# Squares of the first three FFN groups moved to ScalarE, and w_out rounded in pieces of two blocks

## The chip, the core and the metric

The kernel runs on one core of a Trainium2 chip. The metric is the device time of one execution in microseconds. The kernel before was run three times: 516.62, 516.91 and 517.46 us, median 516.91. One further execution was profiled; its time is 516.3 us, and the span from its first to its last instruction, which every time in the profile refers to, is 514.5 us. The five engines are named as in the profile: PE is TensorE (PEld its weight loads), DVE is VectorE, ACT is ScalarE, POOL is GpSimd, SP is SyncE, which issues nearly all DMAs.

## What is computed

An mLSTM cell, step by step over 768 positions for 4 batches and 8 heads of width 40, followed by a feed-forward network whose activation is the squared rectifier:

```python
for t in range(S):
    m_new = np.maximum(f_gate[:, :, t] + m, i_gate[:, :, t])
    f_stab, i_stab = np.exp(f_gate[:, :, t] + m - m_new), np.exp(i_gate[:, :, t] - m_new)
    C = f_stab[:, :, None, None] * C + i_stab[:, :, None, None] * np.einsum('bhd,bhe->bhde', vt, kt)
    n = f_stab[:, :, None] * n + i_stab[:, :, None] * kt
    ...
    y[:, :, t] = o * h_tilde / denom
x = y.transpose(0, 2, 1, 3).reshape(3072, 320)
h = np.maximum(x @ w_in, 0.0)          # w_in: 320 x 2048
out = h * h @ w_out                    # w_out: 2048 x 320
```

The weights w_in and w_out arrive as 8-byte words, of which the kernel makes 4-byte floats on the chip.

## The kernel before

The 3072 rows are 24 tiles of 128 positions, six for each batch. The recurrence is worked in chunks: for a tile s, scores(s) are products of keys and queries on TensorE, weigh(s) makes the decay weights from exponentials on ScalarE (after mask(s) on GpSimd), weighted(s) multiplies scores and weights on VectorE (line 438), attend(s) or attend_turned(s) takes the result times the values on TensorE (lines 461, 513, 522), and normalise(s) divides on VectorE (lines 585 to 593, or 568 to 577) and leaves a tile x_sb. For tiles 0 to 5 turn_rows(s) transposes x_sb on TensorE (line 623) and ScalarE copies the result from PSUM to xT (line 624). For later tiles this goes through DRAM.

The FFN works on groups of two tiles, twelve in all. Groups 0, 1 and 2 are computed in the plain way: ffn1_main and ffn1_rest multiply xT by w_in (lines 645 and 656) in four parts of four blocks of 128 hidden units, two PSUM tiles `h_ps` to a part. relu_half (line 671) takes both to SBUF tiles `r_sb` on ScalarE, and square_half (line 678) squares them on VectorE into `g4`, a part of the group's tile g2. ffn2 multiplies that by w_out (line 685). From group 1 on the second product, and from group 3 on the first, use a scheme with seven products in place of eight (lines 739, 813, 845); in groups from 3 on ScalarE already squares (lines 862, 863). `h_ps` has three buffers in the first phase and five in the second.

The weights are converted by the class Rounding, piece by piece: fetch issues the load of a raw piece on SP's queue, words makes two tiles from its two words on ScalarE (lines 196, 198), join works on these with three VectorE operations (lines 207, 211, 212) and one GpSimd addition that writes the weight (line 216), and then fetches the piece four further on. words runs one piece ahead. There are 10 pieces of w_in, 512 wide, and 16 of w_out, 320 wide. `raw` has four buffers, `mag` and `low` three each.

The order on every engine is the order of the program text: the schedule is written out by hand. The first phase is the loop over u = 0 to 7 at line 956, two steps for each of the tiles 2 to 5; it computes FFN parts of groups 0 and 1, and each step begins with relu_half for the part of the step before. square_half stands after weigh in even steps and at the end of odd ones. The table NEXT says how many pieces are to be joined by the end of each step. Behind the loop stand, in this order, relu_half, square_half and turn_rows(5). The second phase is the loop over `parts` at line 1028, from group 2's first product on, with tile s = 6 + n // 4; LAST does there for n = 0 to 4 what NEXT did. Parts of group 2 come in pairs: both are multiplied, and then relu_half and square_half are called for one and for the other.

Of the kernel before, what the change touches and what calls it, by code (L numbers as in the profile page):

```python
# [9 lines left out]
F32 = mybir.dt.float32  # L10
I32 = mybir.dt.int32
U32 = mybir.dt.uint32
BF16 = mybir.dt.bfloat16
AF = mybir.ActivationFunctionType
ALU = mybir.AluOpType
PSUM = bass.MemoryType.PSUM

P = 128
# [11 lines left out]
def kernel(  # L30
# [27 lines left out]
    nc = tc.nc  # L58
# [7 lines left out]
    DM = H * D  # L66
    DFF = moe_w_in.shape[1]
    NF = DFF // P
# [4 lines left out]
    WG = GT * P  # L73
# [17 lines left out]
    conv = brought.enter_context(tc.tile_pool(name="conv", bufs=2, side="right"))  # L91
# [23 lines left out]
    w_out = consts.tile([P, NF, DM], F32)  # L115
# [27 lines left out]
    def in_words(ap):  # L143
        return ap.bitcast(I32).rearrange("r (c w) -> r c w", w=2)

    win_w, wout_w = in_words(moe_w_in), in_words(moe_w_out)

    rest = win_w[2 * P :].rearrange("p (a two f) w -> p a two f w", two=2, f=P)
    pieces = []
# [8 lines left out]
            ))  # L158
    IN_DONE = (3, 5, 8, 10)
    assert len(pieces) == IN_DONE[-1]  # L160
    pieces += [(w_out[:, fb, :], [(slice(0, P), wout_w[fb * P : (fb + 1) * P])]) for fb in range(NF)]
    NRAW = 4

    class Rounding:
# [11 lines left out]
        def fetch(self):  # L176
            n = len(self.raws)
            if n == len(pieces):
                return
            dst, srcs = pieces[n]  # L180
            raw = conv.tile([P, 512, 2], I32, name="raw", bufs=NRAW)
            self.raws.append(raw)
            for rows, src in srcs:
                to = raw[rows, : dst.shape[1]]
                if len(src.shape) == 4:
                    to = to.rearrange("p (a f) w -> p a f w", a=src.shape[1])
                nc.sync.dma_start(to, src)

        def words(self):
            n = len(self.a)  # L190
            if n == len(pieces):
                return
            w = pieces[n][0].shape[1]
            raw = self.raws[n][:, :w]
            mag = conv.tile([P, 512], F32, name="mag", bufs=3)
            nc.scalar.activation(mag[:, :w], raw[:, :, 1].bitcast(F32), AF.Abs)
            low = conv.tile([P, 512], F32, name="low", bufs=3)
            nc.scalar.activation(low[:, :w], raw[:, :, 0].bitcast(U32), AF.Copy, bias=2.0, scale=2.0 ** -51)
            self.a.append((mag, low))

# [67 lines left out]
    st = {}  # L268
# [51 lines left out]
    def load_o(s):  # L320
        b, c = divmod(s, NB)
        r, (s0, s1) = next((r, (a, z)) for r, (a, z) in enumerate(RUNS) if a <= s < z)
        if s == s0:
            st["og", r] = ld.tile([P, 4, H, D], F32, name="og")
        og = st.setdefault(s, {})["og"] = st["og", r][:, s - s0]
        nc.sync.dma_start(og, o_gate[b, :, c * P : (c + 1) * P, :].rearrange("h p d -> p h d"))
# [338 lines left out]
    def relu_half():  # L665
        if "half" in st:
            hs, g4 = st.pop("half")
            rs = []
            for h in hs:
                rs.append(ffn.tile([P, 2, WG], F32, name="r_sb", bufs=4))  # L670
                nc.scalar.activation(rs[-1][:], h[:], AF.Relu)
            st.setdefault("relu", []).append((rs, g4))

    def square_half():
        if st.get("relu"):
            rs, g4 = st["relu"].pop(0)
            for i, r in enumerate(rs):
                nc.vector.tensor_tensor(g4[:, :, i, :], r[:], r[:], op=ALU.mult)

    def ffn2(g, j, part):  # L680
        if part == 0:
# [212 lines left out]
    load_part(0, 0)  # L894
    load_part(0, 1)
    fetch(2)
    make_consts()
    load_part(1, 0)
    load_part(1, 1)
    load_part(0, 2)  # L900
    fetch(1)
    load_o(0)
    load_o(1)
    load_part(1, 2)
    fetch(1)
    idle(12)
    transposes(0)
# [16 lines left out]
    ffn = ctx.enter_context(tc.tile_pool(name="ffn", bufs=2))  # L924
# [27 lines left out]
    rounding.step()  # L952


    NEXT = (5, 8, 10, 11, 13, 15, 17, 19)
    for u in range(8):
        s = 2 + u // 2
        relu_half()
        if u % 2 == 0:
            if u == 0:  # L960
# [10 lines left out]
            if u == 2:  # L971
                mask(s + 1)
                rounding.join()
                rounding.join()
                weigh(s + 1, masked=True)
                rounding.words()
            else:
                weigh(s + 1)
                square_half()
        else:  # L980
# [7 lines left out]
            if u == 3:  # L988
                square_half()
# [10 lines left out]
            rounding.words()  # L1000
            ffn1(u // 4, u % 4)
            square_half()
        if u < 4:
            load_o(4 + u)
        while rounding.done < NEXT[u]:
            rounding.step()
    relu_half()
    square_half()
    turn_rows(5)
# [12 lines left out]
    for g in range(1, NG):  # L1022
        parts += [(2, g, i) for i in range(4)]
        if g + 2 < NG:
            parts += [(1, g + 2, i) for i in range(4)]
    LAST = (21, 23, 25, 25, 26)
    assert LAST[-1] == len(pieces)
    for n, (which, g, i) in enumerate(parts):
        s, at = 6 + n // 4, n % 4
# [46 lines left out]
        if fast:  # L1076
            (ffn1_close if i % 2 else ffn1_open)(g, i // 2)
            if at == 2:
                do(scale_q, s + 1)
        elif which == 1:  # L1080
            ffn1_main(g, i)
            if i % 2 == 0:
                held = st["half"]
            else:

                both = held, st["half"]
                for more, half in enumerate(both):
                    ffn1_rest(g, i - 1 + more, half[0])
                for half in both:
                    st["half"] = half  # L1090
                    relu_half()
                    square_half()
        elif g == 0:
            ffn2(g, *divmod(i, 2))
        else:
            ffn2_fast(g, i)
# [13 lines left out]
        if n < 5:  # L1110
            while rounding.done < LAST[n]:
                rounding.step()
# [30 lines left out]
```

## Time and profile before

| what | us |
|---|---|
| time, median of three runs | 516.91 |
| span of the profiled execution | 514.5 |
| VectorE squares, line 678, 24 of 128x512 | 18.6 |
| ScalarE relus, line 671, 24 of 128x512 | 12.7 |
| ScalarE words, lines 196 and 198, 26 each | 29.3 |
| VectorE rounding, lines 207, 211, 212, 26 each | 43.9 |
| GpSimd additions, line 216, 26 | 27.6 |
| landing of a 320 KB piece of w_out, median | 3.4 |

These are busy times over the whole span. They say how much work of each kind there is, not what it costs: an engine's work adds to the span only where TensorE or the end of the program waits for it. In the list of instructions in order of time a row gives the start, the length, the engine, the line, the operation, the tiles written and read, the shapes and, in brackets, how long the engine stood idle before it and what ended that. The first relu of line 671 starts at 44.1 us and the last square of line 678 ends at 125.4 us.

### The profile page before, as it was taken

What the parts mean: (1) busy time and instruction counts of PE and PEld (TensorE: products, weight loads), DVE (VectorE), ACT (ScalarE), POOL (GpSimd) and SP (SyncE); (2) the same over time, 40 slices, a digit from 0 to 9 for tenths busy, and PEclk for the clock granted to TensorE, in tenths of its full rate; (3) what the DMA queues carried; (4) which work ended last, traced back from release to release, by engine and by line L of the source; (5) the groups of instructions that cost most, each with busy time, mean ns of one, the idle gap of its engine ahead of it and who ended that gap; (6) DMA issues with size and microseconds to landing.
All of it is one profiled execution on the core that took longest, in us unless ns stands there. A gap on an engine that the chain in (4) does not pass through costs nothing.

```text
span 514.5 us, 11947 instructions
## 1 busy us (share of the span) xinstructions
PE 504.2 (98%) x4649; PEld 462.4 (90%) x4649; DVE 367.6 (71%) x678; ACT 238.1 (46%) x496; POOL 117.1 (23%) x146
## 2 busy tenths in 40 slices
PE   9989999999999999999999999999999999999997
PEld 4867878886698999999999999999999999999997
DVE  8589988969979776677777776677667766544441
ACT  3766667642522642571551581550771651432400
POOL 3345733233314113112112112112112121020000
PEclk9997999999999999999999999999999999999999
DMA  9999599787485786685685685685665352100000
GB/s 191 220 219 194 155 164 204 178 183 145 121 162 102 169 151 118 163 162 109 161 157 114 164 155 118 166 172 96 169 131 99 109 120 74 51 8 29 0 27 27
DMA packets 238360, 67.64 MB, mean 131 GB/s; under 512 B 185728, under 2 KB 232832, under 8 KB 238304
## 3 DMA queue, kind: packets, MB, share of 16 engines
q1 hardware_dynamic: 238208, 66.68, 61.0%
q8 instruction: 37, 0.61, 0.5%
q10 hardware_dynamic: 96, 0.20, 0.1%
q14 instruction: 19, 0.16, 0.1%
HBM read 54.56 MB, written 17.86 MB: 141 GB/s over the span
## 4 chain that ended last, share of the span: by engine, by line
PE 89%; DVE 4%; DMA 2%; ACT 2%; issue 2%; SPq 1%; DVEq 0%
PE h_ps L739 33%; PE h_ps L813 23%; PE h_ps L845 7%; PE h_ps L645 5%; PE tp L423 4%; PE numT L522 3%; PE h_ps L685 3%; PE hp L461 2%; PE numT L513 2%; PE h_ps L656 1%; PE tp L411 1%; PE dC L454 1%; PE A_ps L352 1%; DMA num_rows<-tn 1%; PE dC L532 1%
## 5 line engine op out<-in xcount | busy, mean ns | idle before, releaser
L361 POOL TENSOR_SCALAR_AFFINE_SELECT A_bc<-A_bc 128x1024 f32<-128x1024 f32 x22 | 26.3, 1197 | 207.9 <-ACT kq L371 152.8
L739 PE MATMUL h_ps<-T,S 128*128 128x160 f32 x352 | 51.4, 299 | 0.0
L739 PE MATMUL h_ps<-w_out,g 128*128 128x160 f32 x336 | 49.2, 303 | 0.0
L371 ACT ACTIVATE kq<-A_bc 64x512 f32<-64x512 f32 x30 | 18.9, 628 | 65.2 <-DMA A_bc<-a_rows 65.0
L739 PEld LDWEIGHTS h_ps<-T,S 128*128 128x128 f32 x352 | 49.0, 190 | 0.0
L385 ACT ACTIVATE A_bc<-A_bc,b_T 128x128 f32<-128x128 f32 x144 | 44.1, 389 | 8.7 <-POOL A_bc L361 8.2
L739 PEld LDWEIGHTS h_ps<-w_out,g 128*128 128x128 f32 x336 | 46.1, 190 | 1.1
L645 PE MATMUL h_ps<-xT,w_in 128*128 128x256 f32 x192 | 45.9, 395 | 0.6 <-ACT xT L624 0.6
L645 PEld LDWEIGHTS h_ps<-xT,w_in 128*128 128x128 f32 x192 | 37.1, 198 | 6.6 <-ACT xT L624 0.9
L755 DVE TENSOR_TENSOR y_sb<-y_sb,h_ps 128x160 f32<-128x160 f32 x44 | 14.0, 319 | 38.5 <-PE h_ps L739 38.5
L813 PE MATMUL h_ps<-xT,w_in 128*128 128x128 f32 x288 | 40.6, 284 | 0.0
L826 ACT COPY r_sb<-h_ps 128x512 f32<-128x512 f32 x18 | 10.5, 584 | 63.0 <-PE h_ps L813 62.9
L813 PE MATMUL h_ps<-xs,w_in 128*128 128x128 f32 x288 | 38.0, 275 | 0.0
L813 PEld LDWEIGHTS h_ps<-xT,w_in 128*128 128x128 f32 x288 | 34.9, 191 | 2.8 <-issue 0.5
L845 PE MATMUL h_ps<-xT,w_in 64*128 64x128 f32 x432 | 36.9, 280 | 0.0
L845 PEld LDWEIGHTS h_ps<-xT,w_in 64*128 64x128 f32 x432 | 33.4, 187 | 2.2
L813 PE MATMUL h_ps<-xs,WS 128*128 128x128 f32 x288 | 35.1, 275 | 0.0
L813 PEld LDWEIGHTS h_ps<-xs,w_in 128*128 128x128 f32 x288 | 35.1, 192 | 0.0
L813 PEld LDWEIGHTS h_ps<-xs,WS 128*128 128x128 f32 x288 | 33.6, 192 | 0.0
L850 DVE TENSOR_TENSOR r_sb<-r_sb,h_ps 128x512 f32<-128x512 f32 x18 | 12.4, 687 | 26.0 <-PE h_ps L845 25.7
L739 PE MATMUL h_ps<-w_out,g_c 128*128 128x160 f32 x192 | 28.0, 302 | 0.0
L423 PE MATMUL tp<-kqT 40*128 40x128 f32 x384 | 27.0, 280 | 0.0
(167 smaller groups left out, 1071.2 us busy)
## 6 DMA issues: line engine op xcount, KB each, us to landing
A_bc<-a_rows SPq DMA_DIRECT2D x22, 512.0 KB, 4.6
raw<-in_moe_w_out_dram SPq DMA_DIRECT2D x16, 320.0 KB, 3.4
num_rows<-tn SPq DMA_DIRECT2D x18, 256.0 KB, 3.5
kq<-num_rows SPq DMA_DIRECT2D x72, 64.0 KB, 2.3
kqT<-kq_rows SPq DMA_DIRECT2D x34, 128.0 KB, 3.2
raw<-in_moe_w_in_dram SPq DMA_DIRECT2D x8, 512.0 KB, 5.5
kq<-in_k_dram SPq DMA_DIRECT2D x24, 160.0 KB, 4.9
va<-in_v_dram SPq DMA_DIRECT2D x24, 160.0 KB, 5.2
```

Source lines behind the costliest of these rows:

```text
L361: nc.gpsimd.affine_select(A[:], A[:], compare_op=ALU.is_ge, fill=-1e30, base=0, pattern=[[0, H], [1, P]], channel_multiplier=-1,)
L371: nc.scalar.activation(e[rows], st[s]["A"][0][rows, PR * i : PR * (i + 1), :], AF.Exp)
L385: nc.scalar.activation(d["W"][:, i * n + h, :], A[i][:, h, :], AF.Exp, bias=b_T[:, b, c, i * n + h : i * n + h + 1],)
L423: nc.tensor.matmul(sc[i][:, j, :], lhsT=d["kT"][rows, j, :], rhs=d["qT"][rows, j, :], start=True, stop=True,)
L522: nc.tensor.matmul(numT[i][halves[g], e, :], lhsT=va_w[s % NKQ][:, h * D1 : h * D1 + DP], rhs=d["P"][h % 2][:, h // 2, :] if s < KQ_SQ els ...
L645: nc.tensor.matmul(hs[i][:, n, :], lhsT=w_in[:, a, fb * P : (fb + 1) * P], rhs=xT[:, :, a, :], start=(n == 0 and a == 0), stop=False,)
L685: nc.tensor.matmul(o_ps, lhsT=st["g2", g][:, fb, j * P : (j + 1) * P], rhs=w_out[:, fb, :], start=(fb == 0), stop=(fb == NF - 1),)
L739: nc.tensor.matmul(to, lhsT=lhsT[:, p], rhs=rhs[:, p, :], start=(start and p == 0), stop=(p == NPAIR - 1), skip_group_check=True,)
L755: add = lambda to, a, b: nc.vector.tensor_tensor(to, a, b, op=ALU.add)
L813: nc.tensor.matmul(to[:, n, :], lhsT=lhsT[:, 4 * q + n, :], rhs=rhs, start=(start and n == 0), stop=True, skip_group_check=True,)
L845: nc.tensor.matmul(to[:, n, :], lhsT=w_in2[rows, 4 * q + n, :], rhs=rhs, start=False, stop=True, skip_group_check=True,)
L850: tt(U2[:], U2[:], Y[:], op=ALU.add)
```

## The change

relu_half writes the rectified values straight into `g4`, the tile that is to hold the squares, instead of into `r_sb`. square_half then squares all of `g4` in place by one ScalarE instruction of 128x1024, where two VectorE instructions of 128x512 squared `r_sb` into it. The places at which both are called stay. This holds for the three groups that use these functions.

The pieces of w_out take two blocks of 128 rows each, so there are 8 of 640 columns instead of 16 of 320. The buffers raw, mag and low grow from 512 to 640 columns. The tables NEXT and LAST are written for the new count: by the end of the first loop 15 of 18 pieces are joined (before, 19 of 26), and the last is joined at n = 2 of the second loop (before, at n = 4).

```diff
-    pieces += [(w_out[:, fb, :], [(slice(0, P), wout_w[fb * P : (fb + 1) * P])]) for fb in range(NF)]
+    pieces += [
+        (
+            w_out[:, fb : fb + 2, :].rearrange("p a d -> p (a d)"),
+            [(slice(0, P), wout_w[fb * P : (fb + 2) * P].rearrange("(a p) c w -> p a c w", p=P))],
+        ) for fb in range(0, NF, 2)
+    ]
+    WIDE = 2 * DM
...
-            raw = conv.tile([P, 512, 2], I32, name="raw", bufs=NRAW)
+            raw = conv.tile([P, WIDE, 2], I32, name="raw", bufs=NRAW)
...
-            mag = conv.tile([P, 512], F32, name="mag", bufs=3)
+            mag = conv.tile([P, WIDE], F32, name="mag", bufs=3)
...
-            low = conv.tile([P, 512], F32, name="low", bufs=3)
+            low = conv.tile([P, WIDE], F32, name="low", bufs=3)
...
             hs, g4 = st.pop("half")
-            rs = []
-            for h in hs:
-                rs.append(ffn.tile([P, 2, WG], F32, name="r_sb", bufs=4))
-                nc.scalar.activation(rs[-1][:], h[:], AF.Relu)
-            st.setdefault("relu", []).append((rs, g4))
+            for i, h in enumerate(hs):
+                nc.scalar.activation(g4[:, :, i, :], h[:], AF.Relu)
+            st.setdefault("relu", []).append(g4)
...
         if st.get("relu"):
-            rs, g4 = st["relu"].pop(0)
-            for i, r in enumerate(rs):
-                nc.vector.tensor_tensor(g4[:, :, i, :], r[:], r[:], op=ALU.mult)
+            g4 = st["relu"].pop(0)
+            nc.scalar.activation(g4, g4, AF.Square)
...
-    NEXT = (5, 8, 10, 11, 13, 15, 17, 19)
+    NEXT = (5, 8, 10, 11, 12, 13, 14, 15)
...
-    LAST = (21, 23, 25, 25, 26)
+    LAST = (16, 17, 18, 18, 18)
```

## The prediction

> **What bounds the kernel now.** First the busy shares and the forty slices of the page. TensorE's matmul row is full nearly everywhere, so the span is TensorE's own work plus the places where it waits; what the other engines are given or spared counts only there.
>
> ```profile
> PE 504.2 (98%) x4649; PEld 462.4 (90%) x4649; DVE 367.6 (71%) x678; ACT 238.1 (46%) x496; POOL 117.1 (23%) x146
> PEld 4867878886698999999999999999999999999997
> DVE  8589988969979776677777776677667766544441
> ```
>
> The weight-load row (PEld) shows the gaps better than the matmul row, whose ends are modelled: slices 4 to 12 (39 to 155 us) have holes, the later ones hardly any. The change acts between 44 and 128 us, in slices 4 to 10. So second I read the time-ordered list of weight loads there; in brackets stands the idle time before a row and what ended it.
>
> ```profile
> 65.75 0.73 PEld L656 LDWEIGHTS h_ps<-xT,w_in 64*128 64x128 f32 x8 [0.33 <-issue]
> 68.01 0.31 PEld L623 LDWEIGHTS tp<-ident,x_sb 128*128 128x128 f32 x3 [1.54 <-ACT r_sb L671]
> ...
> 99.53 3.32 PEld L645 LDWEIGHTS h_ps<-xT,w_in 128*128 128x128 f32 x16 [0.16 <-ACT xT L624]
> ...
> 126.20 0.42 PEld L513 LDWEIGHTS numT<-kq,C 40*64 40x64 f32 x14 [1.50 <-DVE A_bc L438]
> ```
>
> Only two gaps in this stretch exceed 0.5 us: before turn_rows(3) at 68.01, and at 126.20. Gaps of 0.33 us ended by "issue" stand at every such change of matmul shape and are normal. Third, VectorE's list, to see who made those gaps:
>
> ```profile
> 60.16 2.35 DVE L678 TENSOR_TENSOR g<-r_sb 128x512 f32<-128x512 f32 x2
> 62.44 0.85 DVE L207 TENSOR_SCALAR mag<-mag 128x320 f32<-128x320 f32 x1
> 63.33 0.92 DVE L211 TENSOR_SCALAR mag<-mag 128x320 int32<-128x320 int32 x1
> 64.28 0.49 DVE L212 SCALAR_TENSOR_TENSOR mag<-raw,mag 128x320 int32<-128x320 int32 x1
> ...
> 67.93 0.20 DVE L593 COPY x_sb<-x_sb 128x64 f32<-128x64 f32 x1
> ...
> 122.27 3.16 DVE L678 TENSOR_TENSOR g_c<-r_sb 128x512 f32<-128x512 f32 x4
> 125.46 1.29 DVE L438 TENSOR_TENSOR A_bc<-tp,A_bc 128x512 f32<-128x512 f32 x2
> ```
>
> VectorE runs without a pause from 60.16 to 68.1: two squares, one rounding piece, then normalise(3), whose last copy (67.93) frees the transposes of turn_rows(3). The profile puts that gap down to ScalarE's L671, but those relus ended at 68.05 by chance; the data waited for is x_sb. At 125.46 weighted(7) stands behind four squares, which themselves waited for relus; TensorE's numT needs the PSUM bank that weighted(7) frees. Both gaps are thus VectorE's queue, with squares in it.
>
> **What the Trainium skill says.** "ScalarE: Activation LUTs", section What ACT_TABLE_LOAD costs: an ACTIVATE with immediate operands takes 186 ns + 0.833 ns per element, and neighbours overlap by some 93 ns. For 1024 elements this gives 1039 ns; the trace has the square of L863 at 1043. "SBUF — State Buffer", section SBUF: two separate sides: VectorE and GpSimd share a port pair as an exclusive lock, and the later one blocks. The trace agrees: L211 takes 0.33 us at 119.83, but 0.92 at 63.33, where it ends just after GpSimd's L480 (63.19 to 64.07). "TensorE: Matmul & The Clock Gate", section What's actually happening: TensorE's clock falls to half after an idle window of about 3.4 us. The trace shows a half-clock stretch from 42 to 48.8 us, after weight loads had paused for 1.38 us at 38.5, so here less than a whole idle window preceded it.
>
> ```profile
> 42.00:44.00 2.00, 2.00 (x12) 2.00 (x12) 1.70 (x4) 2.00 (x9) 0.00 (x0) 0.50 1.16 287
> ```
>
> (The column after the engines is the granted clock: 0.50.)
>
> **The change part by part.** The order of instructions on TensorE is the same before and after; on ScalarE no table load is added.
>
> Removed from VectorE: 24 L678, 12.9 + 5.7 = 18.6 us by the two groups. Removed from the queue ahead of normalise(3): 2.35 us; ahead of weighted(7): 3.16 us plus their wait for the relus.
>
> Added to ScalarE: 12 squares of 128x1024 at 1.045 us, 12.5 us. Rounding of w_out: 320-wide ACTIVATEs follow each other every 0.39 us, 512-wide every 0.57, so 0.00092 us per element and 0.69 for 640: 32 x 0.39 = 12.5 becomes 16 x 0.69 = 11.0. VectorE's three operations together step by 1.13 us at 320 and 1.52 at 512, so 1.78 at 640: 16 x 1.13 = 18.1 becomes 8 x 1.78 = 14.2, where no lock lengthens them. GpSimd's joining add: 0.89 at 320, 1.34 at 512, about 1.6 at 640, 14.2 becomes 12.8. On SP 16 fetches become 8, each with twice the bytes; a bare issue is 0.34, so the queue is spared 2.7 us. All of this lies beside TensorE's work except at three places:
>
> 1. *turn_rows(3), gain.* Without the two squares VectorE goes from L472 (ends 60.2, set by TensorE's dC) straight to a 640-wide piece. Alone that takes 1.8 us, under the lock perhaps 3.1 (the 320-wide one took 2.26 instead of 1.13, and up to two GpSimd operations may be in the way). normalise(3), 3.4 us before, starts at 62 to 63.3 instead of 64.7 and ends by 66.7. TensorE can first use it at 66.81 (last L656 load ends 66.48, plus the normal 0.33). Gain 68.01 - 66.81 = 1.20 at most; if the lock costs everything, 0. I take 1.20.
>
> 2. *xT of tile 5, loss.* After the loop relu_half and square_half stand ahead of turn_rows(5). Before, ScalarE ran two relus and then the copy that ffn1 of group 2 waits for:
>
> ```profile
> 98.02 1.09 ACT L671 ACTIVATE r_sb<-h_ps 128x512 f32<-128x512 f32 x2 [2.33 <-PE h_ps L656]
> 99.00 0.48 ACT L624 COPY xT<-tp 128x384 f32<-128x384 f32 x1
> ```
>
> The relus cannot start earlier, since they waited for TensorE. Now the square (1.045) lies between, and it waits for the relus' end, so the 0.09 overlap is lost there but had again after it: the copy ends at 100.55 instead of 99.48, and TensorE, which already waited 0.16 for it, starts L645 about 1.05 later. Nothing else is queued that TensorE could do first. Loss 1.05; bounds 0.95 and 1.25.
>
> 3. *weighted(7), gain.* Before it now stand rounding piece 18, whose words ScalarE finishes by about 115.3 (relus from 109.7; two relus, square, two relus, square = 4.2, then two 640-wide words 1.4), and normalise(6), which waits for the num_rows loads (116.0). Both are done by 119, and scores(7) end on TensorE at 119.9. So L438 runs at 120 to 121.2, well before 124.5, where numT is first asked for. Its other input, ScalarE's exponentials, ends at 115.3 + 2.45 = 117.8. Gain 1.50, lower bound 1.2, upper 1.75 (part of the 0.44 gap before it).
>
> Other waits that squares lengthen on ScalarE have room: relus before which it idled 1.3 to 2.3 us (74.40, 83.52) take a square of 1.05; at 90.19 the relu comes 0.9 later, but TensorE asks for its bank at 93.5. With five banks in group 2, squares between relus hold a bank 1 us longer, asked for at 111.9 at the earliest. The fetches of 640 KB issued from 49 to 59 us put up to 1.3 MB more ahead of A_bc of tile 5, at 200 GB/s up to 6.5 us in all but only the last one or two still in flight, 1.6 to 3 us; weigh(5) feeds scores at 84, so that is hidden. After 128 us VectorE is again tied to TensorE, so the later gap near 165 moves along unchanged.
>
> Sum: -1.20 + 1.05 - 1.50 = -1.65 us on the profiled span of 514.5, to 512.85. The same execution counts 516.3 as its time, 1.8 more; the three runs give 516.62 to 517.46, median 516.91. I apply the difference to the median: **515.3**. The bounds of the three terms add up to -2.0 and +0.05, 514.9 to 517.0; the upper end is the lock case below. With at least 0.8 of the first gain kept, the forecast's own range is 514.9 to 516.2.
>
> **Rivals.** *The lock eats the first gain.* For it: VectorE's pieces are twice as wide and GpSimd has L397, L475 and L480 to do in just that stretch. Against: 2.35 us of squares, themselves lengthened by the lock (1.29 elsewhere), go. Then -0.45, 516.5. *The clock halves again (the slower side).* The new wait of about 1.05 + 0.16 us at 99.5 falls where weight loads already have 0.33 gaps. If TensorE's idle share in some window passes what the throttle tolerates, half clock follows for as long as the earlier stretch, 6.8 us, and costs half, 3.4 us: 518.7. Against: 1.54 us idle at 66.5 and 1.94 around 125 did not set it off; the pause of 1.38 at 38.5 did, after a thinner stretch. It decides from an idle time near 1.4 us. *The square is hidden after all*, because ScalarE's relus or the copy come out shorter: -2.7, 514.2; nothing speaks for it. The change surely does what it says, as the order of instructions shows.
>
> **How the numbers follow.** Forecast 0.66, hidden square 0.06, lock 0.16, half clock 0.08, some other delay through the bigger fetches or ScalarE's fuller queue 0.04 (slower). A measurement of this kernel tells 0.2% (1.0 us) from no change. So faster 0.72, same 0.16, slower 0.12. The range 514.4 to 517.0 holds the forecast and the lock case and leaves out the half clock.
>
> **What would show it.** Right: the gap before L623 near 67 is 0.3 to 0.5, that before numT near 125 is below 0.5, and the one before L645 near 98.5 is about 1.2, ended by ScalarE's xT. Wrong: no change at 67 with long L207 and L211 ahead of it; a second stretch at clock 0.50; or a new gap elsewhere between 44 and 128 us ended by ScalarE.

## The result, and the profile after

The changed kernel took 513.44 us (median of 4 executions, 512.99 to 514.51), beside 517.18 us for the kernel before in the same comparison: ratio 0.9932, 95% interval 0.9913 to 0.995. Ten more executions in a later comparison gave 513.72 and 0.9944 (0.9922 to 0.9965). The forecast was 515.3 with a range of 514.4 to 517.0: the direction is right, but the gain is 2.9 to 3.7 us where 1.65 was forecast. The profiled execution took 512.99 us, its span is 511.2.

The busy shares and two rows of the forty slices of the changed kernel:

```profile
PE 502.6 (98%) x4648; PEld 460.9 (90%) x4649; DVE 347.0 (68%) x630; ACT 248.7 (49%) x492; POOL 112.7 (22%) x138
PEld 4878888787798999999999999999999999999997
DVE  8588966564879767667768777667768666644341
```

VectorE lost 20.6 us of busy time and ScalarE gained 10.6. PE's busy time even fell by 1.6, about what 3.4 us less of half clock give back. The weight loads of the changed kernel at the three places of the sum (lines moved: L629 was L623, L651 was L645, L519 was L513):

```profile
64.89 0.31 PEld L629 LDWEIGHTS tp<-ident,x_sb 128*128 128x128 f32 x3 [0.90 <-issue]
...
97.50 3.32 PEld L651 LDWEIGHTS h_ps<-xT,w_in 128*128 128x128 f32 x16 [1.25 <-ACT xT L630]
...
122.48 0.43 PEld L519 LDWEIGHTS numT<-kq,C 40*64 40x64 f32 x16 [0.44 <-issue]
```

Before, the brackets read 1.54, 0.16 and 1.50. So the first pause shrank but did not close, the second opened by 1.09, and the third closed. The copy's delay in ScalarE's list is the one forecast, relus, then the square, then xT:

```profile
94.90 1.09 ACT L675 ACTIVATE g<-h_ps 128x512 f32<-128x512 f32 x2 [1.55 <-PE h_ps L662]
96.02 1.06 ACT L681 ACTIVATE g<-g 128x1024 f32<-128x1024 f32 x1
96.98 0.46 ACT L630 COPY xT<-tp 128x384 f32<-128x384 f32 x1
```

VectorE's list ahead of turn_rows(3), with GpSimd's row that matters:

```profile
57.70 0.49 DVE L478 TENSOR_TENSOR C_sb<-dC,bdm 128x328 f32<-128x328 f32 x1
58.10 1.03 DVE L213 TENSOR_SCALAR mag<-mag 128x640 f32<-128x640 f32 x1
59.17 0.92 DVE L217 TENSOR_SCALAR mag<-mag 128x640 int32<-128x640 int32 x1
60.13 1.24 DVE L218 SCALAR_TENSOR_TENSOR mag<-raw,mag 128x640 int32<-128x640 int32 x1
...
62.08 1.54 POOL L222 TENSOR_TENSOR w_out<-mag,low 128x640 int32<-128x640 int32 x1
62.18 1.47 DVE L592 TENSOR_TENSOR dm<-dm,num 128x8 f32<-128x8 f32 x1
...
64.81 0.20 DVE L599 COPY x_sb<-x_sb 128x64 f32<-128x64 f32 x1
```

Two things are to be seen. L592 works on 8 elements per partition and takes 1.47 us, where the same operation took 0.17 at 65.84 in the kernel before: it starts 0.1 us after GpSimd's L222 and ends with it (63.65 and 63.62). This is the lock that the prediction took from the Trainium skill, page "SBUF — State Buffer", section SBUF: two separate sides; the trace agrees. And L478 (before: L472) ends at 58.2, two microseconds earlier than the 60.2 that the prediction had called fixed. Here lies its error; step 1 of the section on the prediction says in what sense.

How much TensorE was ahead at each place, one profile against the other (start before minus start after):

| place | before | after | ahead |
|---|---|---|---|
| first ffn1, ahead of anything changed | 31.89 | 31.25 | 0.64 |
| ffn1_rest of the step ahead of L472 | 50.34 | 47.86 | 2.48 |
| turn_rows(3) | 68.01 | 64.89 | 3.12 |
| ffn1 of group 2 | 99.53 | 97.50 | 2.03 |
| numT of tile 7, loads after the pause (L522; now L528) | 126.79 | 123.08 | 3.71 |

About 2.5 of the 3.3 us of span come ahead of 50 us. Of these, 0.64 us stand ahead of anything changed, and about 1.7 (half of 3.4) come from a shorter half clock; a comparison of two single executions does not show that the change made them. The half-clock stretch is 3.4 us long instead of 6.8; the granted clock is the third figure from the end in this view of two windows of the changed kernel, and was 0.50 in both of the kernel before:

```profile
42.00:44.00 2.00, 2.00 (x11) 2.00 (x11) 1.85 (x7) 2.00 (x8) 0.63 (x1) 0.50 1.15 288
44.00:46.00 2.00, 2.00 (x9) 1.69 (x8) 1.39 (x3) 2.00 (x5) 1.92 (x3) 0.80 1.48 160
```

### The profile page after: what moved, and what is told of

Same layout as the page of the kernel before. It is cut to its first block, busy times and chain, and to the rows that moved or that the text cites. A ratio compares the mean times of both kernels' runs of the same rounds, so it can differ in the third digit from the quotient of the medians.

```text
span 511.2 us, 11842 instructions
## 1 busy us (share of the span) xinstructions
PE 502.6 (98%) x4648; PEld 460.9 (90%) x4649; DVE 347.0 (68%) x630; ACT 248.7 (49%) x492; POOL 112.7 (22%) x138
## 4 chain that ended last, share of the span: by engine, by line
PE 85%; DVE 8%; ACT 2%; issue 2%; DMA 2%; SPq 1%; POOL 0%; DVEq 0%; POOLq 0%; ACTq 0%
PE h_ps L742 32%; PE h_ps L816 21%; PE h_ps L848 7%; PE h_ps L651 6%; PE tp L429 4%; PE h_ps L688 3%; PE numT L528 3%; PE numT L519 2%; PE h_ps L662 2%; DVE mag L217 2%; PE hp L467 1%; DMA A_bc<-a_rows 1%; PE A_ps L358 1%; PE dC L538 1%; ACT g_c L391 1%
## 5 line engine op out<-in xcount | busy, mean ns | idle before, releaser
L651 PE MATMUL h_ps<-xT,w_in 128*128 128x256 f32 x192 | 44.5, 386 | 1.6 <-ACT xT L630 1.6
L651 PEld LDWEIGHTS h_ps<-xT,w_in 128*128 128x128 f32 x192 | 36.1, 193 | 7.3 <-ACT xT L630 2.0
L545 DVE STREAM_TRANSPOSE tn<-numT 128x256 f32<-128x256 f32 x36 | 15.9, 449 | 21.2 <-PE numT L528 21.2
L444 DVE TENSOR_TENSOR A_bc<-tp,A_bc 128x512 f32<-128x512 f32 x36 | 23.1, 684 | 9.5 <-PE tp L429 9.5
```

The costliest lines, as they stand in the source:

```text
L444: nc.vector.tensor_tensor(t, d["sc"][i], d["W"][:, heads, :], op=ALU.mult)
L545: nc.vector.transpose(to[:, 2 * i : 2 * i + 2], numT[i][:, :2, :].rearrange("p c t -> p (c t)"))
L651: nc.tensor.matmul(hs[i][:, n, :], lhsT=w_in[:, a, fb * P : (fb + 1) * P], rhs=xT[:, :, a, :], start=(n == 0 and a == 0), stop=False,)
```

## The experiments

### Halves of the change, and the early half clock

Four theories stood at first: the squares carry the gain and the pairs are beside it; the pairs carry a good part; the half clock comes from TensorE's pause near 39 us but is hidden in the kernel before by VectorE's queue; or it costs 2 to 3.4 us there too. The first kernel has the squares on ScalarE and 16 pieces of w_out, the second the pairs and the squares on VectorE. The other two fill TensorE's pause with products that write the same values a second time, in the kernel before and in the changed one:

```diff
-            for j in range(PR):
+            for j in (*range(PR), *(range(PR) if s == 2 else ())):
                 nc.tensor.matmul(
                     hi[:, 2 * j : 2 * j + 2, :] ...
```

> The squares of groups 0 to 2 on ScalarE in place, w_out still rounded in 16 pieces of 320. Theory A (the squares in VectorE's queue are what cost, and the pairing of w_out is beside it): nearly all of the gain, 0.9925 to 0.9945 of before. Rival B (the pairing of w_out, with fewer VectorE and ScalarE instructions and earlier fetches, gives a good part): at most half of the gain, 0.996 or more.

> w_out rounded two blocks at a time, squares still on VectorE out of the tiles of relus. Theory A: within 1 us of before, since VectorE's queue ahead of normalise(3) is not shorter (the 640-wide piece is longer than the 320-wide one) and four squares still stand ahead of weighted(7): 0.998 to 1.001. Rival B: 0.996 or less.

> The kernel before, with attend(2)'s eight products of qT and C done twice (same result), which fills TensorE's pause of 1.38 us at 38.5 us. Theory C (TensorE's stretch at half clock from 42 us follows from that pause, and in the kernel before VectorE's queue to normalise(3) hides nearly all that it costs): the stretch is gone, and the time is lower by no more than 0.5 us. Rival D (the stretch costs its 6.8 us at half clock in the kernel before too): lower by about 2 to 3.4 us. If the stretch stays, the pause is not its cause.

> The changed kernel with the same filling. Theory C: no execution has the long stretch at half clock, so times lie at the lower end of the changed kernel's, 512.5 to 513.5, 0.3 to 1 us below its median, and scatter less. Rival D: the changed kernel gains as much as the kernel before does by the same filling.

| kernel | us | ratio to before | interval |
|---|---|---|---|
| squares alone | 514.96 | 0.9951 | 0.9926 to 0.9977 |
| pairs alone | 519.43 | 1.0035 | 1.0019 to 1.005 |
| before, pause filled | 516.87 | 0.9986 | 0.9969 to 1.0003 |
| changed, pause filled | 513.35 | 0.9921 | 0.9892 to 0.995 |

Each ratio is to executions of the kernel before in the same comparison; their median was 518.01 us in this one, and 516.6 to 516.9 in the later ones.

The squares carry the gain. The pairs alone lose 1.0 to 2.6 us by the interval, where no loss was expected: the 640-wide piece comes on top of the squares in VectorE's queue, and the pause at turn_rows(3) grows to 3.93 us. With the squares gone, whether the pairs add anything lies within the intervals (0.9951 against 0.9932 and 0.9944).

Filling the pause moves the half clock in the kernel before (in its profile to 52 and 127 us), and its gain cannot be told from none; 15 of the 22 executions lie at 515.6 to 517.5 us and 7 at 519.2 to 520.6, and what sets the 7 apart was not found. In the changed kernel the profile has no half clock, and the time is that of the changed kernel. The two filled kernels still differ by 3.5 us in the medians, so the early stretch alone is not the gain.

### Which squares count

Three kernels put single squares back or over. The condition is on n, the number of the FFN part: (0, 1) as shown, or (8, 9, 10, 11) for group 2. In the changed kernel the same condition sends parts 0 and 1 back to VectorE:

```diff
             hs, g4 = st.pop("half")
+            n = st["n"] = st.get("n", -1) + 1
+            if n in (0, 1):
+                for i, h in enumerate(hs):
+                    nc.scalar.activation(g4[:, :, i, :], h[:], AF.Relu)
+                st.setdefault("relu", []).append((None, g4))
+                return
             rs = []
...
             rs, g4 = st["relu"].pop(0)
+            if rs is None:
+                nc.scalar.activation(g4, g4, AF.Square)
+                return
```

The fourth swaps two lines behind the loop of the changed kernel:

```diff
     relu_half()
-    square_half()
     turn_rows(5)
+    square_half()
```

> The changed kernel with one line moved: turn_rows(5) stands ahead of the last square_half after the loop, so that ScalarE copies xT of tile 5 before it squares part 7. If step 2 of the prediction is right (the square between relus and copy costs TensorE 1.05 us), the gap of 1.25 us before the first ffn1 of group 2 (97.5 us in the changed kernel) falls to about 0.2 and the time is 1.0 us below the changed kernel's: about 512.4, ratio to the kernel before 0.990 to 0.991. Rival: the square is needed just as soon by what follows (the next relus or ffn2 of group 1), and the gap only moves: then as the changed kernel, 0.993.

> The kernel before with the squares of parts 0 and 1 alone on ScalarE; the other ten parts and the pieces of w_out as before. About 4.7 us leave VectorE's queue between 46 and 68 us. Theory Q: VectorE's queue alone sets the end of that stretch, so that TensorE's wait at turn_rows(3) goes and the stretch before it shortens too: gain 1.5 to 2.5 us, 515.0 to 516.0, ratio about 0.996, and no gap over 0.6 us at turn_rows(3). Theory P (the prediction's: VectorE is held to TensorE's time at L472, only the squares after it count): 1.2 us or less, ratio 0.9977 or more. Theory K (the gain ahead of 49 us is a shorter stretch at half clock): no more than P when executions with one granted clock are compared.

> The kernel before with the squares of group 2 alone (parts 8 to 11) on ScalarE. If step 3 of the prediction is right, weighted(7) no longer stands behind four squares on VectorE, the gap of 1.5 us before numT near 126 us falls below 0.5, and the time falls by 1.5 us (1.2 to 1.75): ratio 0.9966 to 0.9977, about 516.0. If the later gap near 166 us (1.1 us, ended by the same line L438) grows by what is won, the ratio is 1.0.

> The changed kernel with the squares of parts 0 and 1 back on VectorE, all else as changed. Theory Q: about 4.7 us come back into VectorE's queue ahead of normalise(3), which now also holds a 640-wide rounding piece: the gap at turn_rows(3) grows from 0.9 to over 2.5 us, and the time by 2 to 4 us: 515.5 to 517.5, ratio about 0.998. Theory P: at most the 1.2 us of step 1, 514.7, ratio 0.9955.

| kernel | us | ratio to before | interval |
|---|---|---|---|
| changed, copy of xT ahead of the square | 512.47 | 0.9919 | 0.9894 to 0.9943 |
| before, parts 0 and 1 moved | 514.38 | 0.9938 | 0.9919 to 0.9958 |
| before, group 2 moved | 515.87 | 0.9985 | 0.9972 to 0.9998 |
| changed, parts 0 and 1 back | 519.47 | 1.0047 | 1.0022 to 1.0072 |

Two parts of twelve, two squares each on VectorE, carry most of the gain: 0.42 to 0.81% of 517 us is 2.2 to 4.2 us, against 1.20 in the prediction. Putting them back costs 6 us and makes the kernel slower than before. The two together have about 4.7 us of VectorE time in the kernel before, so moving them back costs more than they take. The weight loads show why; first the kernel before with the two parts moved, then the changed kernel with them back:

```profile
66.20 0.31 PEld L623 LDWEIGHTS tp<-ident,x_sb 128*128 128x128 f32 x3 [0.33 <-issue]
```

```profile
69.40 0.50 PEld L629 LDWEIGHTS tp<-ident,x_sb 128*128 128x128 f32 x3 [3.50 <-issue]
70.23 1.78 PEld L429 LDWEIGHTS tp<-kqT 40*128 40x128 f32 x16 [0.33 <-issue]
```

With the parts moved there is only the normal 0.33 at turn_rows(3). With them back TensorE waits 3.50 us, and then the 16 loads of L429 take 1.78 us instead of 0.97: TensorE is at half clock from 68.2 to 75.1. The forecast for this kernel, 515.5 to 517.5, left that out and was too low.

Group 2 alone closes the pause ahead of numT, as forecast (its bracket reads 0.44 there), and by the trace wins 1.68 us at that place. The timed gain is 0.1 to 1.4 us. That the time shows less than the trace is left open. The copy first closes the gap of 1.25 us again:

```profile
97.36 3.32 PEld L651 LDWEIGHTS h_ps<-xT,w_in 128*128 128x128 f32 x16 [0.16 <-ACT xT L630]
```

### What a long pause costs beyond itself

Dummy transposes ahead of turn_rows(3), into the bank that it fills next, keep TensorE busy while x_sb is late. They are 14 in the kernel with parts 0 and 1 back and 8 in the kernel before; their results are overwritten.

```diff
         tp = ps_at.tile([P, 3, P], F32, name="tp", tag="at")
+        for k in range(14 if s == 3 else 0):
+            nc.tensor.transpose(tp[:, k % 3, :], ident[:], ident[:])
         for a in range(3):
```

> The kernel with parts 0 and 1 back on VectorE (the run before this one, 519.5 us, pause of 3.5 us at turn_rows(3) and then half clock for 6.8 us), and 14 more transposes of the identity into the bank that turn_rows(3) is about to fill, some 2.3 us of TensorE work that nobody reads, inside that pause. VectorE's queue and the time at which x_sb is ready stay. Theory H (part of the loss is the half clock that follows a long pause): no half clock at 69 to 76, the time falls by about 3.4 us to 516, the granted clock is 0.993. Theory W (the wait itself is the loss, the clock is chance): time and clock stay, 519.5 and 0.99.

> The kernel before with 8 transposes of the identity at the same place, some 1.3 us of TensorE work inside its pause of 1.5 us there. Theory H: executions of the kernel before with 0.990 or less (19 of 80 so far, medians 518.2 to 520.3) have the half clock at this place too; they go, the median falls by 0.5 to 1.0 us, ratio 0.998 to 0.999. Theory W: ratio 1.000, and executions at 0.990 and less stay as frequent.

The first took 517.46 us, ratio 1.0019 (1.0008 to 1.0031), beside 1.0047 without the fill. Its weight loads:

```profile
66.25 1.51 PEld L629 LDWEIGHTS tp<-ident 128*128 128x128 f32 x14 [0.33 <-issue]
69.43 0.37 PEld L631 LDWEIGHTS tp<-ident,x_sb 128*128 128x128 f32 x3 [1.67 <-DVE x_sb L598]
69.92 0.97 PEld L429 LDWEIGHTS tp<-kqT 40*128 40x128 f32 x16
```

x_sb is ready at the same time (69.43 and 69.40), but the half clock behind it is gone, and the span is 2.6 us shorter. So in these traces a long pause costs twice: the wait, and TensorE's slower work after it. The size is 2.0 us in the medians and 1.4 by the ratios, whose intervals overlap, not the 3.4 expected. Without the fill 10 of 11 executions have a granted clock of 0.990 or less, with it 9 of 22, so the fill did not remove every half clock.

In the kernel before the fill gave 516.58, ratio 0.9994 (0.9982 to 1.0006). One of 22 executions is at 0.990 or less, where the kernel before has 32 of the 157 executions of all comparisons. The long half clocks seem to go, but they were too few to move the median: the 0.5 to 1.0 us expected did not come.

### Was the profile of before a typical one?

> The changed kernel unchanged, for its granted clocks and a second profile. If its gain is that the wait at turn_rows(3) is short, no execution is at 0.990 or less (the kernel before: 19 of 80), the time is 513.4 again, and the pause there again between 0.3 and 1.6 us. If the shorter early stretch at half clock (3.4 us instead of 6.8) belongs to the change, most executions are at 0.997 or more; if it was chance, most are at 0.993.

> The kernel before unchanged, for another profile. Theory T (the execution that the forecast was worked out from was a lucky one of the kernel before): the pause at turn_rows(3) is 2.0 to 2.4 us here instead of 1.54, as in the two runs that share its first 68 us (2.21, and about 2.1 with the extra transposes counted), and the time is nearer to 517. Rival (it was typical, and the gain beyond the forecast has another place): 1.4 to 1.7 us.

> As the run before it, a further profile of the kernel before: theory T 2.0 to 2.4 us in most of the three, with half clock after it where it is 2.2 or more; rival 1.4 to 1.7.

> As the two before it, a further profile of the kernel before.

> The changed kernel unchanged, a third profile: the pause at turn_rows(3) 0.5 to 0.9 us again and no half clock after it; the gap before the first ffn1 of group 2 1.25 us, and before numT near 122 to 125 us below 0.5 us. Whether the stretch at half clock ahead of 49 us is 3.4 or 6.8 us is open.

The weight loads around turn_rows(3) in the second, third and fourth profile of the kernel before, in that order:

```profile
65.52 0.73 PEld L656 LDWEIGHTS h_ps<-xT,w_in 64*128 64x128 f32 x8 [0.33 <-issue]
68.37 0.38 PEld L623 LDWEIGHTS tp<-ident,x_sb 128*128 128x128 f32 x3 [2.12 <-ACT r_sb L671]
...
71.09 5.41 PEld L645 LDWEIGHTS h_ps<-xT,w_in 128*128 128x128 f32 x16 [0.22 <-issue]
```

```profile
64.66 0.73 PEld L656 LDWEIGHTS h_ps<-xT,w_in 64*128 64x128 f32 x8 [0.33 <-issue]
67.99 0.31 PEld L623 LDWEIGHTS tp<-ident,x_sb 128*128 128x128 f32 x3 [2.60 <-issue]
```

```profile
67.02 0.73 PEld L656 LDWEIGHTS h_ps<-xT,w_in 64*128 64x128 f32 x8 [0.33 <-issue]
68.79 0.31 PEld L623 LDWEIGHTS tp<-ident,x_sb 128*128 128x128 f32 x3 [1.04 <-issue]
```

With the profile of the prediction, and the three of the changed kernel:

| profile | us | half clock at 39 to 50 us | L656 (now L662) starts | turn_rows(3) starts | pause | half clock after it |
|---|---|---|---|---|---|---|
| before, the one predicted from | 516.3 | 6.8 | 65.75 | 68.01 | 1.54 | none |
| before, second | 522.3 | 6.8 | 65.52 | 68.37 | 2.12 | 6.8 |
| before, third | 518.96 | 3.4 | 64.66 | 67.99 | 2.60 | 3.4 |
| before, fourth | 517.41 | 10.2 | 67.02 | 68.79 | 1.04 | none |
| changed, the result | 512.99 | 3.4 | 63.26 | 64.89 | 0.90 | none |
| changed, second | 516.3 | 6.8 | 65.99 | 67.05 | 0.33, then 0.56 inside | none |
| changed, third | 516.53 | 6.8 | 66.60 | 67.67 | 0.33 | none |

The second profile's 522.3 us is longer than any of the 157 executions in the comparisons (515.2 to 520.4), so it is an extreme one. The second and third profile of the changed kernel also have a half clock of 3.4 us at 14 to 18 us, ahead of anything changed: their first ffn1 starts at 32.34 and 32.79 us, against 31.25 in the first, and this part of their later arrival is not the change's.

In the kernel before TensorE comes to turn_rows(3) over a span of 2.4 us (64.66 to 67.02), depending on how long the early half clock lasted, but goes on within 0.8 us (67.99 to 68.79): VectorE decides. An execution with a short half clock wins nothing by it, it only waits longer, and then pays with a new half clock. In the changed kernel turn_rows(3) starts 1.1 to 1.6 us after L662 each time, of which 1.06 is L662 itself and the normal gap (before: 1.8 to 3.3), so that a shorter half clock becomes time. That the one profile was a lucky one is half true: two of four have a pause over 2 us and the half clock, two have not. In the second profile L645's 16 loads after the pause take 5.41 us instead of 3.32, and TensorE falls from 0.36 us behind the first profile to 3.61 behind at the L656 after it: that half clock costs 3.25 us. In the third the same two rows are 6.86 us apart instead of 5.22, so that its shorter one costs 1.64.

The granted clock over a whole execution fits. At 0.996 and above 8 of 14 executions of the changed kernel have a median of 512.96; those at 0.992 and 0.993 have 514.5 (4), those at 0.989 and 0.990 515.73 (2), where none had been expected. One of these two is the second profile, which has 10.2 us of half clock and none of it at turn_rows(3). For the kernel before these are 516.0 (32 of 157), 516.9 (93) and 518.0 (32). Like for like the gain is 2.3 to 3.0 us, and from the middle class to the upper the changed kernel wins 1.5 us, the kernel before 0.9. The classes of the changed kernel are small. Why it is at full clock more often was not found; its second and third profile have the long early stretch, so it is not that the change removes it.

### Squares ahead of the point that the prediction held fixed

This kernel is the one with parts 0 and 1 moved, with `n in (0,)` as the condition: only the squares that stand at 46.9 us, well ahead of L472, leave VectorE.

> The kernel before with the squares of part 0 alone on ScalarE. On VectorE they stand at 46.9 us, well ahead of L472 (59.7). The prediction held VectorE to TensorE's dC at L472: theory P, time as before, ratio 1.000, pause at turn_rows(3) as before (1.0 to 2.6 us). Theory Q: VectorE has no pause from 46.9 to 68.1 us, so that these squares are worth as much there as those of part 1: x_sb is ready 1.0 to 2.3 us earlier, and the time falls by 1.0 to 2.0 us, ratio 0.996 to 0.998.

It took 515.77 us, ratio 0.9983 (0.9971 to 0.9996). Those squares are worth 0.2 to 1.5 us, where 1.0 to 2.0 were expected and the prediction's step gives nothing. VectorE's list of this kernel, in which no row from 48 us to x_sb has a bracket:

```profile
58.71 0.49 DVE L472 TENSOR_TENSOR C_sb<-dC,bdm 128x328 f32<-128x328 f32 x1
59.11 2.39 DVE L687 TENSOR_TENSOR g<-r_sb 128x512 f32<-128x512 f32 x2
...
66.92 0.19 DVE L593 COPY x_sb<-x_sb 128x64 f32<-128x64 f32 x1
```

L472 moved from 59.74 to 58.71 and x_sb from 67.93 to 66.92, each by 1.0 us. Here it was not held to dC, whose products end at 57.59, 1.1 us before L472. TensorE, with a half clock of 3.4 us from 33 to 36 us in this execution instead of one from 42 to 48, came early and waited 2.64 us.

### Versions that take the rest of the pauses

Two more edits to the changed kernel: the copy first, as above, and in step u = 3 the rounding piece joined after normalise(3); and both of these with the hi products twice, which fills the pause near 39 us.

```diff
-            rounding.join()
+            if u != 3:
+                rounding.join()
             normalise(s)
+            if u == 3:
+                rounding.join()
```

> The changed kernel with turn_rows(5) ahead of the last square_half, and with the rounding piece of step u=3 joined after normalise(3) instead of before it. The first saved about 1 us (512.5). The second takes about 3 us of VectorE from the queue ahead of turn_rows(3), so that its pause of 0.9 to 1.5 us goes to 0.3: 511.3, ratio to the kernel before 0.988. Rival: the piece, joined 3 us later, now stands ahead of weighted(4) or holds back its successor's fetch, and the pause comes back there: 512.5, 0.991.

> The kernel with both moves (turn_rows(5) ahead of the last square_half, the piece of step u=3 after normalise(3); 511.1 us) and attend(2)'s hi products issued twice, which writes the same values again, so that TensorE is not idle in the pause of 1.2 us near 39 us. In that kernel executions at a granted clock of 1.000 took 510.2 and at 0.993 512.8. If the half clock ahead of 49 us comes from that pause and VectorE no longer hides it, most executions are at 0.996 or more and the median is 510.3 to 511; if the fill delays what it stands ahead of, or the half clock comes elsewhere, 511 or more.

The first took 511.06 us, ratio 0.9893 (0.9863 to 0.9923), the second 510.26 us, ratio 0.9866 (0.9848 to 0.9885), its four executions all at a granted clock of 1.000. Weight loads of the second:

```profile
63.78 0.31 PEld L629 LDWEIGHTS tp<-ident,x_sb 128*128 128x128 f32 x3 [0.33 <-issue]
...
95.34 3.32 PEld L651 LDWEIGHTS h_ps<-xT,w_in 128*128 128x128 f32 x16 [0.16 <-ACT xT L630]
```

Both pauses are closed. Filling the pause near 39 us, which gave nothing that could be told in either kernel at first, gives 0.8 us in the medians here; the intervals of the two versions overlap, so that it is likely and not shown that the fill counts once nothing on VectorE hides it. The second is the best version here, some 3 us below the changed kernel.

## Why the prediction was wrong in size

**Step 1, turn_rows(3): the term that was mis-sized.** "Gain 68.01 - 66.81 = 1.20 at most" failed as a bound, and with it "VectorE goes from L472 (ends 60.2, set by TensorE's dC)". The two parts alone measured 2.2 to 4.2 us. For the one execution that it was read from the step holds, but by a coincidence:

```profile
58.65 1.06 PE L454 MATMUL dC<-vw,kq 128*128 128x82 f32 x8
59.32 0.49 DVE L467 TENSOR_TENSOR num<-hi,eA_T 128x328 f32<-128x328 f32 x1
59.74 0.50 DVE L472 TENSOR_TENSOR C_sb<-dC,bdm 128x328 f32<-128x328 f32 x1
```

L472 follows L467 with no bracket, so VectorE waited for nothing; but dC's products end at 59.71, only 0.03 us before it starts. Queue and operand came together. In the third profile, where the early half clock was 3.4 us, they did not:

```profile
57.57 1.06 PE L454 MATMUL dC<-vw,kq 128*128 128x82 f32 x8
59.74 0.49 DVE L472 TENSOR_TENSOR C_sb<-dC,bdm 128x328 f32<-128x328 f32 x1
```

dC is done 1.1 us before L472. There VectorE's queue alone decides, and the squares of part 0 in it count as well as those of part 1: from 46.9 to 68.1 us it is one stretch. Of the four, only the fourth profile, the one with the longest half clock, has dC holding L472, and the bracket names it:

```profile
61.02 0.50 DVE L472 TENSOR_TENSOR C_sb<-dC,bdm 128x328 f32<-128x328 f32 x1 [0.39 <-PE dC L454]
```

So the step took TensorE as it ran in one execution, with 6.8 us of half clock ahead, for what TensorE always does; and it gave a price to the pause but none to a half clock that follows a longer pause. An estimate from the four profiles shows the size of both: the pauses less the normal 0.33 us are 1.21, 1.79, 2.27 and 0.71 us, and the half clocks after them cost 0, 3.25, 1.64 and 0. The sums run from 0.7 to 5.0 us with a mean of 2.7, where the prediction has 1.20.

**The lock.** The range of 1.8 to 3.1 us for the 640-wide piece was just passed (3.2 us, from L213 at 58.10 to L589 at 61.29). normalise(3) took 3.7 us instead of the 3.4 assumed, with 1.47 for L592 in it. That the gain was larger all the same is VectorE's earlier start. The rival "the lock eats the first gain" may be true of some of the gain: with the piece behind normalise(3), and all else alike, the time went from 512.47 to 511.06 in the medians, with overlapping intervals.

**Step 2, xT of tile 5: right.** 1.09 us in the profile, and 1.0 to 1.3 us in the medians when the copy goes first (512.47 against 513.44 and 513.72), though the intervals of the times overlap.

**Step 3, weighted(7): right in the trace.** The pause is gone and 1.68 us are won at the place; the timed run of group 2 alone shows less, at most 1.4.

**"The later gap near 165 moves along unchanged": wrong by 0.4.** It is 1.10 to 1.36 in four profiles of the kernel before and 0.68 or 0.69 in three of the changed one.

**The rival of a half clock: right in kind, wrong in place.** It was put at the new wait at 99.5 us with a price of 3.4. That wait of 1.25 never set one off in the three profiles. The half clock that mattered, of 3.25 and 1.64 us, was in the kernel before, in two of its four profiles; none of the three profiles of the changed kernel has it at turn_rows(3), where its pauses are short. Three profiles do not show how often it still comes. The profile that the prediction read shows none of it, nor could its three times.

As an estimate, the terms add up to a gain of 2.2 - 1.05 + 0.1 + 0.4 = 1.7 to 4.2 - 1.05 + 1.7 + 0.4 = 5.3 us; the 2.9 to 3.7 measured lie within, and the runs pin them no closer. A pause of 0.6 to 1.2 us near 402 to 409 us, in all three profiles of the changed kernel and (1.4 us) in one of four of the kernel before, takes some of it back; what makes it was not tried.

## What to carry to other kernels

A row with no bracket waited for nothing: before a time in a queue is taken as fixed, follow the queue back until a row names who held it, and count all the work from there. Then look how far ahead the row's operand was ready, since a shorter queue gains only that much before it has to wait: 0.03 us in one execution here, 1.1 in another. The cost of a late operand is not its pause alone, since TensorE may run at half clock after it; and one profile shows one outcome of that, so that a second and third profile of the unchanged kernel are worth more than a finer sum on the first.

## What was not expected of the hardware

At turn_rows(3) pauses of 2.12, 2.21, 2.60, 2.64, 3.50 and 3.93 us, in six profiles of five kernels, were each accompanied by a half clock of 3.4 or 6.8 us; pauses of 1.67 us and less, in nine profiles at this place, by none. The Trainium skill, page "TensorE: Matmul & The Clock Gate", section What's actually happening, has a window of 3413 ns that runs freely. The lengths agree with that, 3.4, 6.8 and 10.2 us being one, two and three of it. So do the places: in the nine profiles with two half clocks between 10 and 135 us the second starts 27.3, 34.1 or 75.1 us after the first, which are 8, 10 and 22 such windows. But that the clock falls only after an idle window of 3.4 us does not agree, as a pause of 2.1 us was followed by it here, and so were the pauses of 1.2 to 1.4 us near 39 us, in all 15 profiles that have one.

The length of the pause alone does not decide it. Ahead of numT a pause of 2.13 us was followed by no half clock in the second profile of the kernel before, and one of 1.79 us was, in the kernel before with the pause near 39 us filled. How the pause lies on the windows may decide; that was not tested.

An operation of VectorE on 8 elements per partition took 1.47 us in the changed kernel, and 1.27 and 1.01 in the one with parts 0 and 1 back, instead of 0.17 to 0.34, while GpSimd ran an addition or a select of 1.1 to 1.5 us; each ended 0.02 or 0.03 us after GpSimd's. Where tiny operations run beside GpSimd's work, GpSimd's rows have to be read for their cost, too.
